# A fused band-attention and feed-forward kernel: softmax sums of the first four tiles from a column of ones in V, a later issue of the range-check reads, and a new set of order tables

## The chip, the cores and the metric

The kernel runs on one core of one Trainium2 chip. The metric is the device time of one execution in microseconds (us), the median of several runs. The engines are named as in the profile: PE (TensorE, matrix products), PEld (its weight loads), DVE (VectorE), ACT (ScalarE), POOL (GpSimd), and SP, whose queue issues nearly all DMAs.

## The reference, cut to what matters

```python
def _attn_ref(q, k, v, n_global, n_local):          # q, k, v: (4, 8, 768, 64) float32
    scores = scale * np.matmul(q, k.transpose(0, 1, 3, 2))
    is_global = pos[None, :] < int(n_global)         # 8
    is_local = (rel >= 0) & (rel < int(n_local))     # 96
    dist = np.where(is_global & ~is_local, float(n_local), np.abs(rel))
    scores = scores - slopes[:, None, None] * dist   # slopes 2 ** -(h + 1)
    scores = np.where(is_global | is_local, scores, -1e9)
    a = np.exp(scores - np.max(scores, axis=-1, keepdims=True))
    a = a / (np.sum(a, axis=-1, keepdims=True) + 1e-09)
    return np.matmul(a, v)

def _moe_ref(x, g_ln, w_ch1, w_ch2):                 # x: (4, 768, 512); 512 -> 2048 -> 512
    xn = (x - mu) / np.sqrt(var + 1e-06) * g_ln
    return x + np.maximum(xn @ w_ch1, 0.0) @ w_ch2   # weights arrive as float64
```

## The kernel before

The 3072 tokens are cut into 24 tiles of 128. Tiles 0 to 3 are the first tile of each batch: they see one block of keys and are computed in float32. Tiles 4 to 23 see two blocks and are computed in float16 pairs (a high and a low part). Two tiles make a chunk c of 256 tokens for the feed-forward part: chunk 0 is tiles 0 and 1, chunk 1 is tiles 2 and 3, and so on. From chunk 3 on (`EVEN`) the second product is computed by seven block products in place of eight.

**Names.** For tile t and group of heads g the tasks are: `S` scores (PE), `R` mask and minimum (DVE), `E` exponentials (ACT), `tp`/`pl` transpose of the weights on PE and its copy to SBUF (tiles 0 to 3), `ph`, `pl`, `pt` split and transposing DMA (other tiles), `P` weights by values (PE), `Z`/`X` divisor and division (ACT, DVE), `B`, `A`, `W`, `C` the statistics and normalisation, `xt`, `xh`, `xl` transpose and the two halves of xT (tiles 0 to 3), `xa` the same by a DMA (other tiles). `F` is the first product of the feed-forward part (in the trace PE writes `f` from `xT` and `w1h`, `w1l`), `G` and `N` the second (`f` from `w2`, and `m`). A weight piece n of 16 passes through `wb` (load), `wr` (ACT, `less`), `ws` and `ww` (DVE, int32), `wu` (`w1h` or `w2h`) and `wl` (DVE, `w1l` or `w2l`). Pieces 0 to 7 are w1, two pieces for every two F of each chunk; pieces 0 to 3 stand in the room of `w2h` and `w2l` until then, so their `wr`, `ws` and `ww` rows read `w2h<-w2h` and `w2l<-w2l`. `gk` copies 16 keys between tiles (DVE, `kT<-kT`).

**What sets the order.** Every engine works strictly in the order in which its instructions were written. That order comes from a planner (class `Plan`): each task has a cost, a rank and the tasks it waits for, and the planner starts, on each engine, the ready task of lowest rank. Ranks come from the step at which a task is due, plus table entries: `FIRST` and `KINDS` by kind, `SHIFT` by task; `GIVEN` fixes the engine of a task that two engines could do. Where the planner sees PE idle before its time `UNTIL`, it writes filler products (`blank`) of 128x512 that nobody reads; they are there to keep PE at work. The PE order of the steps themselves is fixed by code: four F of chunk 0, two of chunk 1, two of chunk 0 and so on (`TURN`). The eleventh F in that order, F0_12, is the first that needs weight pieces 6 and 7.

**The sum before.** For tiles 0 to 3 an exponential row of one head is one ACTIVATE on ACT with `accum_out=sm`, which puts an ACTIVATION_READ_ACCUMULATOR behind it. One division by the eight sums then makes x.

**The range check.** Near the end the float64 weights are read once more (`again`, 64 reads of 256 KB, tasks `V0` to `V63`), each followed by a DVE pass (`J`, tile `seen`). They share 12 buffers. The result decides whether a general path must run instead.

## Time and profile before

| what | value |
|---|---|
| median of 3 runs | 599.83 us (599.55 to 600.0) |
| the profiled execution | 599.55 us |
| its span, first to last instruction | 597.8 us |
| PE busy | 586.9 us (98%) |
| DVE, ACT, POOL busy | 494.0, 429.3, 154.0 us |
| granted TensorE clock | 1.0 throughout, the 2.4 GHz level |

The profiled execution lies 1.75 us above its span (the launch around the instructions) and 0.28 us below the median. The busy shares are means over stages: DVE is full in the first quarter and has room later, PE is filled with filler products in the first 44 us.

### The profile page before, as it was taken

Reading aid. Unit: us, or ns where it says so; the run is one execution under the profiler, and the core shown is the slowest. Engines: PE = TensorE matmul, PEld = TensorE weight load, DVE = VectorE, ACT = ScalarE, POOL = GpSimd, SP = SyncE. Lnnn points to the kernel's source line nnn. Section 1 sums busy time; section 2 is a strip of 40 time slices with the busy share of each in tenths; the row PEclk is TensorE's granted clock in tenths of the full one; section 3 lists DMA queues with packets and bytes.
Section 4 is the critical chain, followed back from the end, with each engine's and each line's share of the span. In section 5 each row is a group of like instructions: output and inputs, shape, how many; then the busy total and the mean of one; then the engine's idle time right before and its main releaser. Section 6 shows DMA issues by size and latency. Waiting matters only on the chain. (4 is left out here: it accounts for less than half of the span.)

```text
span 597.8 us, 15687 instructions
## 1 busy us (share of the span) xinstructions
PE 586.9 (98%) x5982; PEld 494.9 (83%) x5982; DVE 494.0 (83%) x1207; ACT 429.3 (72%) x1092; POOL 154.0 (26%) x133
## 2 busy tenths in 40 slices
PE   8999999999999999999999999999999999999996
PEld 5768895547956899999999999999999999888885
DVE  3899999989898987887887886877976876699994
ACT  5999697767666897797787698899686675623330
POOL 2322032135363253231330130231330420300100
PEclk9999999999999999999999999999999999999999
DMA  8995989999966848797776789759569646999931
GB/s 218 332 311 134 249 202 271 248 173 194 181 135 124 187 89 147 159 166 159 169 115 127 138 154 169 174 121 175 111 140 170 118 91 72 233 280 278 393 107 39
DMA packets 256754, 105.40 MB, mean 176 GB/s; under 512 B 238372, under 2 KB 238628, under 8 KB 256676
## 3 DMA queue, kind: packets, MB, share of 16 engines
q1 hardware_dynamic: 256672, 104.37, 78.1%
q8 instruction: 48, 0.79, 0.5%
q14 instruction: 30, 0.25, 0.1%
q10 hardware_dynamic: 4, 0.00, 0.0%
HBM read 54.53 MB, written 6.29 MB: 102 GB/s over the span
## 5 line engine op out<-in xcount | busy, mean ns | idle before, releaser
L257 PE MATMUL f<-xT,w1h 128*128 128x256 f16 x1536 | 256.3, 273 | 1.6 <-DMA xT<-xn 0.9
L257 PE MATMUL f<-xT,w1l 128*128 128x256 f16 x768 | 209.3, 273 | 0.0
L257 PEld LDWEIGHTS <-w1h 128*128 128x128 f16 x1536 | 147.3, 98 | 18.0 <-DMA xT<-xn 1.1
L257 ACT ACTIVATE uh<-R 128x896 f16<-128x896 f32 x72 | 67.9, 943 | 51.8 <-DVE R L257 50.3
L257 PEld LDWEIGHTS <-uh 128*128 128x128 f16 x1008 | 96.2, 98 | 10.5
L257 DVE SCALAR_TENSOR_TENSOR R<-f,R 128x128 f32<-128x128 f32 (+1 forms) x216 | 72.1, 334 | 20.6 <-ACT R L257 15.6
L257 PEld LDWEIGHTS <-w1l 128*128 128x128 f16 x768 | 75.1, 98 | 9.6 <-issue 0.7
L257 ACT ACTIVATE T<-T,mn 128x256 f32<-128x256 f32 x160 | 80.0, 500 | 4.3 <-ACT mn L257 0.4
L257 DVE TENSOR_TENSOR ul<-R,uh 128x896 f16<-128x896 f32 x60 | 68.1, 1136 | 17.0 <-ACT uh L257 15.9
L257 POOL TENSOR_TENSOR pn<-T,pn 128x512 f16<-128x512 f32 x37 | 49.9, 1349 | 120.2 <-ACT pn L257 82.4
L257 PE MATMUL m<-w2h,uh 128*128 128x256 f16 x288 | 78.5, 273 | 0.0
L257 PE MATMUL m<-w2l,uh 128*128 128x256 f16 x288 | 78.5, 273 | 0.0
L257 PE MATMUL m<-w2h,ul 128*128 128x256 f16 x288 | 78.5, 273 | 0.0
L257 PE MATMUL m<-t,uh 128*128 128x256 f16 x432 | 78.3, 273 | 0.0
L257 DVE CUSTOM_DVE_ANT_0 T<-s,mask 128x256 f32<-128x256 f32 (+1 forms) x192 | 68.1, 395 | 8.6 <-PE s L257 8.6
L257 PE MATMUL f<-w2h,h 128*128 128x512 f16 x192 | 60.1, 379 | 0.0
L257 PE MATMUL m<-t,ul 128*128 128x256 f16 x216 | 58.9, 273 | 0.0
L257 PE MATMUL s<-kT,qT 128*128 128x128 f16 (+1 forms) x704 | 56.9, 225 | 0.7 <-DVE kT L257 0.7
L257 PEld LDWEIGHTS <-ul 128*128 128x128 f16 x504 | 49.3, 98 | 5.7
L257 ACT ACTIVATE mn<-nm 128x2 f32<-128x2 f32 x80 | 15.8, 198 | 53.2 <-DVE nm L257 52.9
L257 POOL TENSOR_TENSOR rs<-rs,half 128x1 f32<-128x1 f32 x24 | 18.2, 760 | 138.1 <-DVE rs L257 138.0
L257 PEld LDWEIGHTS <-h 128*128 128x128 f16 x288 | 27.3, 98 | 29.7
(144 smaller groups left out, 994.6 us busy)
## 6 DMA issues: line engine op xcount, KB each, us to landing
again<-in_moe_w_ch_dram SPq DMA_DIRECT2D x64, 256.0 KB, 5.1
st<-in_moe_w_ch_dram SPq DMA_DIRECT2D x10, 1024.0 KB, 6.0
vf<-in_v_dram SPq DMA_DIRECT2D x28, 256.0 KB, 3.4
kf<-in_k_dram SPq DMA_DIRECT2D x28, 256.0 KB, 4.0
qf<-in_q_dram SPq DMA_DIRECT2D x24, 256.0 KB, 3.7
out_dram<-x SPq DMA_DIRECT2D x23, 256.0 KB, 3.6
qT<-qT SPq DMA_DIRECT2D x40, 128.0 KB, 3.5
w2h<-in_moe_w_ch_dram SPq DMA_DIRECT2D x3, 1024.0 KB, 6.6
```

Source lines behind the costliest of these rows:

```text
L257: ins = getattr(self.engine, name)(*args, **kw)
```

## The change

Four things are changed.

- `HALVES = 1`. For tiles 0 to 3 the V tile is loaded 65 columns wide per head, POOL writes ones into the last column (`one`), and the product with V gives the sum of the weights as its 65th column. The exponentials lose `accum_out`. The product of each half of the heads has a PSUM tile of its own, and so the divisor (`Za`, `Z`) and the division (`Xa`, `X`) are done in two halves.
- The reads `V12` to `V63` of the range check name the task `J` that frees their buffer and get 2.5 us of slack in the planner, so that they are written later in SP's order.
- The tables `FIRST`, `SHIFT`, `MARGIN`, `GIVEN` and `lag` have new values. The constants `EARLY` and `FAVOR` change too, but PE's planned time starts at 1.5 and is never below `EARLY`, so `FAVOR` is not used.
- `GIVEN`, empty before, names an engine for 62 tasks.

```diff
-HALVES = 0
+HALVES = 1
...
 GIVEN = {
-
+    "mask0_4": "DVE", "mask0_1": "DVE", "mask0_5": "DVE", "mask0_7": "DVE", "mask1_3": "ACT", "mask1_5": "ACT", "mask1_6": "ACT", "wu4": "ACT",
...
-    def __init__(self, lag=0.039):
+    def __init__(self, lag=0.038):
...
-        task(f"V{n_}", "SP", 0.6, lambda n_=n_, tag=tag: read_again(n_, tag), [f"S{B * NT - 1}_1"], rank=1e4 + n_, take={tag: [f"J{n_}"]}, dma=0.8)
+        task(f"V{n_}", "SP", 0.6, lambda n_=n_, tag=tag: read_again(n_, tag), [f"S{B * NT - 1}_1"] + ([f"J{n_ - 12}"] if n_ >= 12 else []), rank=1e4 + n_, take={tag: [f"J{n_}"]}, dma=0.8, slack=2.5 * (n_ >= 12))
```

Of the code that `HALVES` switches on, these lines matter:

```python
act.activation(out=T[:, u, :], in_=T[:, u, :], func=AF.Exp, scale=-1.0, bias=mn[:, h:h + 1])
sums[t, g] = (ps_f if g else ps_v).tile([P, gh, D + 1], F32, tag="f2" if g else "pv", name=f"pv{t}_{g}")
pv, r, x_, sum_ = sums.pop((t, g))[:, :, :D], made["r", t][:, g::2], x[:, g::2, :], made["sum", t] if g else 0.0
act.activation(out=made["r", t][:, g::2], in_=sums[t, g][:, :, D], func=AF.Copy, bias=1e-9)
```

Over the whole main path the change in instruction counts is: PE 7 fillers fewer (66 to 59), 56 of the 59 ahead of the first F against 65 before; on ACT 8 small divisors (`r<-pv`) for 4, `w1h` 4 more, masks of 128x256 5 more, masks of 128x128 4 fewer; on POOL masks 7 to 1, `pn` 37 to 43, `kn` 11 to 7; on DVE `pn` 43 to 37, `kn` 13 to 17, 8 half divisions for 4 whole ones.

ACT's order near its start, where the exponentials of tile 0 stand (`T_0` and `T_1` are its two groups). Before:

```order
L257 ACTIVATE kT_0_174<-tk_167 128x512
L257 ACTIVATE mask_87<-d_158 128x128 x8
L257 ACTIVATE T_0_200,sm<-T_0_200,nm 128x128 x4
L257 ACTIVATE T_1_218,sm<-T_1_218,nm 128x128 x4
L257 ACTIVATE pT_0_251<-tp_0_239 128x512
L257 ACTIVATE r<-sm 128x8
```

And of the change:

```order
L265 ACTIVATE kT_0_171<-tk_164 128x512
L265 ACTIVATE mask_87<-d_160 128x128 x4
L265 ACTIVATE mask_88<-d 128x256 x3
L265 ACTIVATE T_0_200<-T_0_200,nm 128x128 x4
L265 ACTIVATE T_1_214<-T_1_214,nm 128x128 x4
L265 ACTIVATE pT_0_243<-tp_0_238 128x512
```

The exponentials no longer write `sm`; half of the small masks went to DVE, and three of the wide masks came from POOL.

DVE's order ahead of the `w1l` of weight pieces 6 and 7, which F0_12 waits for. Before:

```order
L257 SCALAR_TENSOR_TENSOR h_8_929<-f_0_8_867,h_8_929 128x512
L257 SCALAR_TENSOR_TENSOR st_849<-st_849 128x1024 x2
L257 SCALAR_TENSOR_TENSOR h_10_963<-f_0_10_902,h_10_963 128x512
L257 SCALAR_TENSOR_TENSOR w1l<-w2h,gw,w1h 128x512 x2
L257 SCALAR_TENSOR_TENSOR w1l<-st_849,gw,w1h 128x512 x2
L257 SCALAR_TENSOR_TENSOR h_4_998<-f_1_4_936,h_4_998 128x512
```

And of the change:

```order
L265 TENSOR_TENSOR kn_1_908<-kf_1_756,kn_1_908 128x8x64
L265 SCALAR_TENSOR_TENSOR w1l<-w2h,gw,w1h 128x512 x2
L265 SCALAR_TENSOR_TENSOR h_8_939<-f_0_8_876,h_8_939 128x512
L265 SCALAR_TENSOR_TENSOR h_10_975<-f_0_10_913,h_10_975 128x512
L265 SCALAR_TENSOR_TENSOR qn_945<-qf_2_597,qn_945 128x8x64
L265 SCALAR_TENSOR_TENSOR st_830<-st_830 128x1024
L265 SCALAR_TENSOR_TENSOR w2l<-w2l 128x1024
L265 SCALAR_TENSOR_TENSOR h_4_1011<-f_1_4_949,h_4_1011 128x512
L265 SCALAR_TENSOR_TENSOR w1l<-st_830,gw,w1h 128x512 x2
```

The second pair of `w1l` stands behind `h_4` of chunk 1 now, and behind one int32 pass of a later weight piece (`w2l<-w2l`).

SP's order at the range-check reads, with the transposing DMAs of tile 23 (`pT_1`, `pT_2`) between them. The difference:

```order
L257 DMA_TRANSPOSE pT_1_8430<-pn_1_8365 128x8x128
L257 DMA again_8465<-in_moe_w_ch_dram 128x256
L257 DMA again_8470<-in_moe_w_ch_dram 128x256
L257 DMA again_8473<-in_moe_w_ch_dram 128x256
L257 DMA again_8476<-in_moe_w_ch_dram 128x256
L257 DMA_TRANSPOSE pT_2_8489<-pn_2_8467 128x8x128
```

```order
L265 DMA_TRANSPOSE pT_1_8449<-pn_1_8381 128x8x128
L265 DMA again_8481<-in_moe_w_ch_dram 128x256
L265 DMA again_8488<-in_moe_w_ch_dram 128x256
L265 DMA again_8490<-in_moe_w_ch_dram 128x256
L265 DMA_TRANSPOSE pT_2_8502<-pn_2_8484 128x8x128
```

Three reads stand between the two transposes of the change, four stood there before (the first of each pair is the kernel before, the second the changed one).

## Rows read from the trace of the kernel before

**Rows 1.** Busy time by stage: stretch, its length, busy us (count) of each engine, PEclk, DMA, GB/s.
```profile
10.80:44.71 33.91, 32.61 (x231) 24.74 (x231) 29.84 (x100) 33.03 (x106) 11.83 (x12) 1.00 1.01 312
44.71:72.12 27.41, 27.36 (x254) 24.52 (x254) 26.48 (x35) 21.97 (x36) 4.21 (x3) 1.00 0.78 196
72.12:112.12 40.00, 39.30 (x352) 27.36 (x351) 39.78 (x75) 33.09 (x73) 9.66 (x6) 1.00 0.96 232
```

**Rows 2.** Waits of PE: who waited for whom, us in total, times, longest.
```profile
PE pv L257 <- DMA pT<-pn: 1.0, 2, 0.5
PE f L257 <- DMA xT<-xn: 0.9, 1, 0.9
PE s L257 <- DVE kT L257: 0.7, 1, 0.7
```

**Rows 3.** Timeline of PE before the first F: start, us, instruction, count [idle before].
```profile
42.22 1.89 PE L257 MATMUL blank<-ident 128*128 128x512 f16 x8
...
44.76 0.27 PE L257 MATMUL f<-xT,w1h 128*128 128x256 f16 x1 [0.54 <-DVE xT L257]
```

**Rows 4.** Timeline of ACT, 9 to 46 us.
```profile
9.00 1.69 ACT L257 ACTIVATE mask<-d 128x128 bf16<-128x128 f32 x8
10.80 0.40 ACT L257 ACTIVATE T<-T,nm 128x128 f32<-128x128 f32 x1
11.11 0.19 ACT L257 ACTIVATION_READ_ACCUMULATOR T<-T,nm 128x1 f32 x1
11.21 0.39 ACT L257 ACTIVATE T<-T,nm 128x128 f32<-128x128 f32 x1
...
37.96 1.21 ACT L257 ACTIVATE w2l<-w2l,less 128x1024 int32<-128x1024 uint32 x1
39.06 0.57 ACT L257 ACTIVATE pT<-tp 128x512 f32<-128x512 f32 x1
...
39.86 0.81 ACT L257 ACTIVATE xs<-x,off,rs 128x512 f32<-128x512 f32 x1
...
42.22 0.57 ACT L257 ACTIVATE xT<-tx 128x512 f16<-128x512 f32 x1
...
45.09 1.40 ACT L257 ACTIVATE w1h<-w2l,gw 128x512 f16<-128x512 f32 x2
```

**Rows 5.** Timeline of DVE, 29 to 45 us.
```profile
29.54 1.85 DVE L257 TENSOR_SCALAR w1h<-w2h,gw 128x512 f16<-128x512 f32 x2
...
39.20 3.94 DVE L257 SCALAR_TENSOR_TENSOR w2l<-w2l 128x1024 int32<-128x1024 int32 x2 [0.36 <-ACT w2l L257]
43.06 0.20 DVE L257 RECIPROCAL r<-r 128x8 f32<-128x8 f32 x1
43.41 0.69 DVE L257 CUSTOM_DVE_ANT_1 x<-pv,r 128x512 f32<-128x512 f32 x1
...
44.02 0.69 DVE L257 TENSOR_TENSOR xT<-tx,xT 128x512 f16<-128x512 f32 x1
```

**Rows 6.** Timeline of POOL at the same place.
```profile
38.91 1.90 POOL L257 TENSOR_TENSOR w1h<-w2l,gw 128x1024 f16<-128x1024 f32 x1
```

**Rows 7.** Timeline of DVE, 59 to 73 us.
```profile
59.72 2.32 DVE L257 SCALAR_TENSOR_TENSOR w1l<-st,gw,w1h 128x512 f16<-128x512 f32 x2
...
63.76 2.47 DVE L257 SCALAR_TENSOR_TENSOR w2h<-w2h 128x1024 int32<-128x1024 int32 x2
...
71.07 1.41 DVE L257 SCALAR_TENSOR_TENSOR w1l<-st,gw,w1h 128x512 f16<-128x512 f32 x2
```

**Rows 8.** Timeline of DVE, then of SP's queue, ahead of the wait at 139.6 us.
```profile
135.08 0.68 DVE L257 TENSOR_TENSOR xn<-xs,xn 128x512 f16<-128x512 f32 x1
...
135.79 1.23 SPq L257 DMA_TRANSPOSE xT<-xn  x1
```

**Rows 9.** Timeline of SP's queue, 518 to 523 us.
```profile
518.76 2.75 SPq L257 DMA_DIRECT2D again<-in_moe_w_ch_dram  x4
521.61 1.30 SPq L257 DMA_TRANSPOSE pT<-pn  x1
```

More of the change, by code (lines that the diff above doesn't have):

```diff
@@ L81 @@
 EVEN = 3
-EARLY = -18.5
+EARLY = -20
 LEAD = 4
@@ L90 @@
 VLATE = 0.0
-FAVOR = {"ACT": 36.8, "POOL": -10.6}
+FAVOR = {"ACT": 60.9, "POOL": -11.1}
 LATER = {"ACT": -1.68, "POOL": -0.05}
@@ L95 @@
 TAIL = {"PE": 0.16, "ACT": 0.1, "DVE": 0.09, "POOL": 0.06}
-MARGIN = {"ACT": 0.0126, "DVE": 0.0032, "POOL": 0.091}
+MARGIN = {"ACT": 0.0316, "DVE": 0.0, "POOL": 0.075}
 SPLIT = 190.0
 FIRST = {
[4 rows of a table removed]
[4 rows of a table added]
 }
```

40 rows, old and new, of tables (FIRST, GIVEN, SHIFT) are left out of this document.

## The prediction

> **What bounds the kernel now.** I read the busy time by stage first, then PE's waits, and then the timelines at the places where PE waits. From 44.76 us on PE works on products that count, and it is all but full: after that moment its waits are 0.7 us for a copy of keys, 0.9 us for an xT that a DMA brings, and twice about 0.5 us for a pT, 2.6 us together [rows 2]. So the kernel has two parts. What comes after 44.76 us can shrink by 2.6 us at most, since no product is taken away. What comes before, 44.76 us, ends when DVE has written the second half of xT for tile 1: PE's first F waits for it [rows 3]. In that stretch PE is busy only because fillers stand there; ACT works 33.03 of 33.91 us and DVE 29.84 [rows 1]. The stage behind it matters too: from 44.71 to 112.12 us DVE works 66.26 of 67.41 us [rows 1], and it is DVE that PE then waits for.
>
> **The change up to the first F.** The path is shared by ACT and DVE, so I add up both queues, each from the first exponential or mask to the xT of tile 1. An ACTIVATE's price is the distance to the next start, its length less 0.09 us (10.80 + 0.40 against 11.11); the accumulator read behind it adds 0.10 (11.11 to 11.21) [rows 4].
>
> ACT needs 31.4 us from 10.80 to 42.22 [rows 4]. Gone are 32 accumulator reads. Their price has a lower bound of 0.10 each, 3.2 us, if the exponential keeps its length; the upper bound is the distance of the small masks, 0.20 each (1.69 us for 8), against 0.39 for an exponential with its read, 6.1 us. I take 3.2, since the exponential's own row is the nearest. By the order of ACT's instructions these change as well ahead of the xT of tile 1: two copies of 0.48 fewer (a pT is one), -1.0; three small `r` of 0.1 more, +0.3; one `less` pass more, +1.1; four `w1h` halves more, +2.6; one normalisation `xs` with its offset fewer, -1.0; two wide masks of an estimated 0.3 more, +0.6 [rows 4]. Sum: -0.6 us; with the upper bound -3.5. ACT's half of the xT ended at 42.79 and would end at 42.2, 1.8 us before DVE began its own half at 44.02 [rows 4, 5].
>
> DVE needs 33.55 us from its first mask to 44.02. More: a copy of 0.6, a wide mask of about 0.3, one int32 pass of 1.2, and seven half divisions in place of four whole ones. A whole one costs 0.96 (43.06 to 44.02), of which 0.35 is the reciprocal and its wait; a half I put at 0.35 + 0.31, an estimate with half of the elements, so 4.6 against 3.8, +0.8. Less: the two `w1h` of 1.85, which ACT takes [rows 5]. Sum: +1.05. Then there is POOL. The two int32 passes at 39.20 took 3.94 us, and at 63.76 two of the same shape took 2.47 [rows 5, 7]; beside the slow ones POOL ran `w1h<-w2l` for 1.90 us from 38.91 [rows 6]. That POOL instruction is gone, and six of seven masks on POOL with it: -1.5. DVE's own work is then 0.4 us shorter. It also idles about 4 us in this stretch (29.84 of 33.91, [rows 1]), one of them just ahead of the slow passes and waiting for ACT [rows 5], and of these waits an ACT that is earlier gives some back.
>
> So ACT allows 1.8 us, and DVE allows 0.4 plus what it idles less: DVE sets it. I take 1.3 us for the start of the first F (0.9 of the 4 us of idle time go), with bounds of 0.3 (no wait goes) and 2.5 (ACT far ahead by the upper bound, half of the idle time gone). The order gives one more number to hold against it: 9 fillers fewer stand ahead of the first F, at 0.22 us each (42.22 to 43.95 for 8), so PE may come 1.9 us earlier and no more unless they were hiding waits [rows 3]. The memsets of ones on POOL have no price: four of them, in an engine that works 11.83 of 33.91 us [rows 1].
>
> **The change after the first F.** Three places follow in time.
>
> *F0_12, now at about 72 us.* Its second `w1l` pair ended at 72.48 [rows 7], that is 28.4 us after DVE began the xT of tile 1, and PE came just then. Counted out with 0.60 for a pass of 512 columns, 1.33 for a pair of `w1l` and 1.13 for an int32 pass, DVE's rows between these two points came to 26.6 us before and come to 28.0 now: the half division of tile 3, an int32 pass of another piece and `h_4` of chunk 1 stand in between. The 1.8 us that the trace shows above 26.6 are waits and a POOL pass beside DVE (2.32 us for a pair of `w1l` at 59.72 against 1.41 at 71.07) [rows 7]. With the same 1.8 PE gets there 1.4 us late; with none of them DVE is in time, and PE loses the net two fillers that stand there now, 0.4 us. I take 1.0.
>
> *The key copy at 111.6 us.* DVE's work ahead of it is 2.0 us less than before by the same count (66.3 us from the xT of tile 1, before 68.3). PE comes 1.0 us later. The wait of 0.7 goes [rows 2].
>
> *The xT of chunk 2 at 139.6 us.* `xn` of tile 5 ended at 135.76, its DMA was issued at 135.79 and PE began at 140.50 [rows 8, 2]. What is late next shows here: DVE has 1.2 us more ahead of this `xn` than before, its waits in the same chain (behind two key and value passes) are about 1 us shorter, and PE comes 0.3 us later on balance (1.0 - 0.7). Bounds: the wait stays as it is less 0.3, or grows by 0.9. I take +0.2.
>
> *The end.* PE's second wait of 0.5 us for a pT comes behind four range-check reads, which SP issued in 2.75 us [rows 9]. One of the four is moved behind the pT: 0.7 us sooner, and the wait of 0.5 goes. The first wait stays, since the eight reads ahead of it stay. The later reads move by 2.5 us at most, and nothing but the verdict waits for them. I take -0.5, with bounds of 0 and -1.0.
>
> In between, from 140.5 to 522 us, PE waits for nothing in the trace; DVE gets 3 to 4 us more work there and ACT 8 us less. I take 0, and up to 1.0 lost.
>
> **Sum.** -1.3 + 1.0 - 0.7 + 0.2 - 0.5 = -1.3 us, on the profiled execution of 599.55: 598.25, so 598.2. The median of the runs shown is 0.28 above that execution. A change of under 0.2%, 1.2 us, counts as no change here.
>
> **The Trainium skill on a price.** The Trainium skill, "SBUF — State Buffer", section "Who interferes with whom", says that a DVE instruction with two SBUF inputs and a GpSimd instruction that reads SBUF exclude each other for a whole instruction. The 3.94 us beside 1.90 agree with it. By that rule the six `pn` that go from DVE to POOL relieve DVE of nothing, since POOL's pass holds it up for longer than its own would last; this is rival B below.
>
> **Rivals.**
>
> *A. No change.* The longer chain of the sums (product, divisor, two divisions in place of one) keeps DVE waiting for all its 4 us, F starts 0.3 us earlier, F0_12 costs 1.0, the key copy and the pT give 1.2 back. 599.55 - 0.3 + 1.0 + 0.2 - 1.2 = 599.3. For it: DVE's work does not shrink. Against it: ACT, the fuller of the two [rows 1], gets room.
>
> *B. Slower: DVE falls behind.* From 44.71 to 112.12 us DVE has 1.15 us of room [rows 1], and the change gives it no less work in all. If POOL's added passes hold DVE up, as the pair at 59.72 shows with 0.9 us each, it loses the 1.8 us at F0_12 and as much again ahead of the xT of chunk 2. It decides from the point where DVE loses 1.5 us more than before between the first F and 140 us. Price: -0.3 (first F) + 1.4 + 1.8 - 0.5 = +2.4, 601.9 at the worst and 600.9 with half of the second loss.
>
> *C. Much faster.* The exponentials cost 0.20, the first F starts 2.5 us earlier, F0_12 loses only its fillers, 0.4, and all four waits go, 2.6 less a remainder of 0.6: 599.55 - 2.5 + 0.4 - 2.0 = 595.45.
>
> **Chances and range.** The forecast 0.45, A 0.18, B 0.20, C 0.17. A quarter of the forecast's share lies above 598.35, within 0.2% of the time before. So faster by over 0.2%: 0.33 + 0.17 = 0.50; within: 0.12 + 0.18 = 0.30; slower: 0.20. The range takes in C but for its end and B up to half of its second loss: 595.5 to 600.9. The forecast's own range is 597.2 to 599.0.
>
> **What would show it.** The exponentials of tiles 0 to 3 should follow each other at 0.30 us, or at 0.20 if the upper bound holds. The first F should wait for DVE's xT still, with its dense start near 43.4 us. PE's waits should name `w1l` near 71 us, no `kT`, one xT by DMA of about a microsecond and one pT. The prediction is wrong if the first F starts after 44.4 or before 42.2, or if PE's waits after it are above 3.5 us.

## The result, and the profile after

| | median | ratio to the kernel before, 95% interval |
|---|---|---|
| kernel before, beside it | 600.0 us (599.55 to 601.37, 5 runs) | |
| changed kernel | 605.85 us (604.05 to 607.11, 5 runs) | 1.0093 [1.0077, 1.0109] |

The change makes the kernel slower by 0.9%, 5.6 us, where 1.3 us faster was forecast. Later runs were made on several chips, on which the median of the kernel before lay between 599.7 and 601.4 us; they are compared by their ratio to it.

The profiled execution of the changed kernel took 605.07 us (span 603.3). Its busy time by stage, in the windows of [rows 1], and PE's clock in 2 us windows where it fell:

```profile
10.80:44.71 33.91, 30.48 (x222) 23.12 (x221) 29.84 (x102) 32.13 (x78) 7.64 (x7) 1.00 1.06 314
44.71:72.12 27.41, 26.66 (x247) 23.79 (x245) 23.27 (x35) 20.93 (x36) 3.31 (x3) 1.00 0.76 183
72.12:112.12 40.00, 38.61 (x334) 26.60 (x333) 38.39 (x68) 28.60 (x66) 11.47 (x9) 0.96 0.92 221
...
74.00:76.00 2.00, 1.05 (x5) 0.53 (x6) 2.00 (x4) 0.45 (x1) 0.00 (x0) 0.77 0.76 172
76.00:78.00 2.00, 2.00 (x12) 1.43 (x10) 2.00 (x7) 1.10 (x4) 0.00 (x0) 0.50 1.18 254
78.00:80.00 2.00, 2.00 (x22) 1.75 (x21) 1.39 (x2) 1.55 (x5) 1.06 (x1) 0.88 0.96 335
```

DVE is no longer full behind the first F (23.27 of 27.41 us, 26.48 before), and between 72 and 112 us the clock is no longer 1.00. In 76:78 PE is busy all the time and gets through 12 instructions at the lower level (0.50, 1.2 GHz) where 78:80 shows 22 at 0.88.

PE's waits, as in [rows 2]:

```profile
PE pv L265 <- DVE mv L265: 2.9, 1, 2.9
PE tx L265 <- DVE r L265: 2.6, 1, 2.6
PE f L265 <- DMA xT<-xn: 2.0, 3, 1.0
...
PE f L265 <- DVE w1l L265: 1.2, 1, 1.2
PE s L265 <- DMA qT<-qT: 0.7, 1, 0.7
...
PE f L265 <- ACT w1h L265: 0.2, 1, 0.2
```

The kT wait and both pT waits of [rows 2] are gone. What is new is 2.9 us for `mv`, 2.6 for `r` (it stands before the first F), 2.1 in three waits near 72 us, and two further waits for an xT, 1.0 together, the longer of them far behind the rest:

```profile
234.80 0.39 PE L265 MATMUL f<-xT,w1h 128*128 128x256 f16 x2 [0.75 <-DMA xT<-xn]
```

**Where the time went.** Executions differ by up to 2.2 us in when their first exponential starts, also with the same instructions ahead of it on ACT (9.42 to 11.59 us in the changed kernel and the runs below that keep its order there). So I count from that start, between moments that every trace shows: first F (its first product with `w1l`), first G (first product with `w2`), first F of chunk 2, first product into `m`, start of the last product.

| us | to first F | to first G | to F2_0 | to first m | to the end | sum |
|---|---|---|---|---|---|---|
| before | 34.07 | 45.33 | 50.30 | 64.71 | 387.18 | 581.59 |
| after | 34.74 | 50.07 | 49.42 | 66.95 | 387.14 | 588.32 |
| difference | +0.67 | +4.74 | -0.88 | +2.24 | -0.04 | +6.73 |

Three places lose: a little before the first F, most between first F and first G, the rest between F2_0 and the first m. One gains, 0.88 between first G and F2_0, of which 0.70 is the kT wait that is gone. Each loss has its rows.

*23 to 28 us.* DVE's pair of int32 passes, POOL's pass beside it, and PE:

```profile
23.08 4.07 DVE L265 SCALAR_TENSOR_TENSOR w2h<-w2h 128x1024 int32<-128x1024 int32 x2
23.25 2.81 POOL L265 TENSOR_TENSOR w1h<-w2h,gw 128x1024 f16<-128x1024 f32 x1 [1.79 <-DVE gw L265]
27.90 0.63 PE L265 MATMUL tx<-ident,xs 128*128 128x128 f32 x4 [2.57 <-DVE r L265]
```

This answers to [rows 5, 6]: the pair took 3.94 there beside 1.90 of POOL. The same meeting has only moved, from a place where PE had fillers to one where it waits. The exponentials themselves follow each other at 0.30, as forecast from [rows 4]:

```profile
9.85 2.45 ACT L265 ACTIVATE T<-T,nm 128x128 f32<-128x128 f32 x8
```

*55 to 75 us.* SP's queue, then ACT, DVE and PE:

```profile
55.82 2.26 SPq L265 DMA_DIRECT2D st<-in_moe_w_ch_dram  x2
58.72 1.44 SPq L265 DMA_TRANSPOSE kT<-kn  x1
61.19 4.17 SPq L265 DMA_TRANSPOSE qT<-qn  x1
65.45 1.26 SPq L265 DMA_TRANSPOSE kT<-kn  x1
...
68.91 1.20 SPq L265 DMA_DIRECT2D qT<-qT  x2
...
66.55 0.63 ACT L265 ACTIVATE qn<-qf 128x512 f16<-128x512 f32 x1 [1.73 <-DMA kT<-kn]
68.92 0.63 ACT L265 ACTIVATE kn<-kf 128x512 f16<-128x512 f32 x1 [1.74 <-DMA qT<-qn]
...
70.07 0.69 DVE L265 SCALAR_TENSOR_TENSOR h<-f,h 128x512 f16<-128x512 f32 x1 [3.51 <-ACT h L265]
74.15 1.41 DVE L265 SCALAR_TENSOR_TENSOR w1l<-st,gw,w1h 128x512 f16<-128x512 f32 x2
...
71.97 0.55 PE L265 MATMUL s<-kT,qT 128*128 128x128 f16 x7 [0.75 <-DMA qT<-qT]
73.37 0.39 PE L265 MATMUL f<-xT,w1h 128*128 128x256 f16 x2 [0.20 <-ACT w1h L265]
74.95 0.32 PE L265 MATMUL f<-xT,w1l 128*128 128x256 f16 x1 [1.18 <-DVE w1l L265]
```

The rows read as a chain. Two 1 MB reads (pieces 6 and 13) are issued 1.9 us apart. Behind them stand the transposing DMAs of tile 4: that of its first keys (58.72) lands 7.7 us after its issue, that of its queries takes 4.17 us to issue, and that of its other keys starts only at 65.45. ACT waits twice for the buffers which the first two of these DMAs read; `h` behind it is late; DVE waits 3.51 us for that `h`; so the second `w1l` pair, at 71.07 in [rows 7], begins at 74.15. PE waits for the copies of `qT`, for `w1h` and for `w1l`. In the kernel before the read of piece 13 was issued at 95.12. The link between the read and the slow issue is the firmest part of this chain: in the six traces in which the read stands there (the changed kernel, fillers, POOL to DVE, casts to ACT, gw later, reads back) the queries' transposing DMA takes 3.37 to 4.50 us to issue, and in the nine of the runs below that move the read it takes 1.23 in each.

*184 to 199 us.* DVE, POOL and PE:

```profile
184.27 1.53 DVE L265 TENSOR_TENSOR pn<-T,pn 128x512 f16<-128x512 f32 x1
185.72 1.37 DVE L265 CAST t<-va 128x512 f16<-128x512 f32 x1
187.13 1.53 DVE L265 TENSOR_TENSOR t<-va,t 128x512 f16<-128x512 f32 x1
...
191.05 1.31 DVE L265 CAST kn<-kf 128x512 f16<-128x512 f32 x1
192.39 1.53 DVE L265 TENSOR_TENSOR kn<-kf,kn 128x512 f16<-128x512 f32 x1
193.84 1.64 DVE L265 SCALAR_TENSOR_TENSOR qn<-qf,qn 128x512 f16<-128x512 f32 x1
...
185.21 1.60 POOL L265 TENSOR_TENSOR va<-va,w2h 128x512 f32<-128x512 f32 x1
186.78 1.33 POOL L265 TENSOR_TENSOR va<-va,w2l 128x512 f32<-128x512 f32 x1
...
198.96 0.51 PE L265 MATMUL pv<-vn,pT 128*128 128x64 f16 x12 [2.89 <-DVE mv L265]
```

Six DVE passes of 0.42 to 0.68 us take 1.31 to 1.64 while POOL works on `va`; above the short lengths that is 5.35 us, ahead of the division that releases `pv`.

### The profile page after: what moved, and what is told of

It reads as the page before. It is cut to its first block, busy times and chain, and to the rows that moved or that the text cites. A ratio compares the mean times of both kernels' runs of the same rounds, so it can differ in the third digit from the quotient of the medians.

```text
span 603.3 us, 15657 instructions
## 1 busy us (share of the span) xinstructions
PE 586.4 (97%) x5975; PEld 494.8 (82%) x5975; DVE 507.4 (84%) x1237; ACT 420.4 (70%) x1048; POOL 158.3 (26%) x135
## 5 line engine op out<-in xcount | busy, mean ns | idle before, releaser
L265 POOL TENSOR_TENSOR pn<-T,pn 128x512 f16<-128x512 f32 x43 | 59.5, 1385 | 155.5 <-ACT pn L265 131.2
L265 ACT ACTIVATE uh<-R 128x896 f16<-128x896 f32 x70 | 65.9, 941 | 34.8 <-DVE R L265 34.7
L265 DVE TENSOR_TENSOR ul<-R,uh 128x896 f16<-128x896 f32 x59 | 65.9, 1116 | 15.0 <-ACT uh L265 14.3
L265 ACT ACTIVATE R<-f 128x512 f32<-128x512 f32 x70 | 40.9, 585 | 31.3 <-PE f L265 26.4
L265 POOL TENSOR_TENSOR rs<-rs,half 128x1 f32<-128x1 f32 x24 | 19.8, 824 | 117.9 <-DVE rs L265 105.9
```

The costliest lines, as they stand in the source:

```text
L265: ins = getattr(self.engine, name)(*args, **kw)
```

## The experiments

Most edits change only the place of a task in the finished order (`MOVED`: a task, and the task that it is put behind), or its engine (`ON`), by lists that are applied behind the planner; nothing else moves:

```diff
+        for key, behind in MOVED:
+            row = order.pop([k for _, k, _ in order].index(key))
+            order.insert([k for _, k, _ in order].index(behind) + 1, row)
...
-(lambda fn=fn, engine=engine: fn(engine))
+(lambda fn=fn, engine=ON.get(key, engine): fn(engine))
```

The stages of all runs, counted as above:

| run | ratio [interval] | to first F | to first G | to F2_0 | to first m |
|---|---|---|---|---|---|
| later load | 1.0106 [1.0084, 1.0128] | 35.62 | 47.67 | 50.35 | 68.63 |
| fillers | 1.0134 [1.0111, 1.0157] | 35.61 | 48.15 | 49.99 | 69.83 |
| POOL to DVE | 1.0057 [1.0043, 1.0072] | 37.26 | 48.19 | 49.70 | 65.83 |
| casts to ACT | 1.0080 [1.0061, 1.0099] | 35.62 | 49.19 | 49.72 | 67.97 |
| spread load | 1.0155 [1.0121, 1.0188] | 35.61 | 45.90 | 57.77 | 66.94 |
| gw later | 1.0059 [1.0036, 1.0081] | 33.62 | 48.50 | 49.70 | 68.28 |
| three edits | 1.0074 [1.0049, 1.0099] | 33.46 | 45.72 | 56.77 | 65.76 |
| sums only | 1.0242 [1.0209, 1.0275] | 35.77 | 45.19 | 59.04 | 67.45 |
| three moves | 1.0029 [1.0009, 1.0050] | 33.48 | 47.17 | 49.41 | 69.15 |
| reads only | 0.9999 [0.9979, 1.0019] | 34.47 | 45.29 | 49.79 | 65.18 |
| reads back | 1.0127 [1.0083, 1.0171] | 38.20 | 48.32 | 49.78 | 68.42 |
| all places | 1.0001 [0.9988, 1.0013] | 33.49 | 46.86 | 50.79 | 65.13 |
| all places, reads back | 1.0057 [1.0039, 1.0074] | 41.23 | 46.50 | 50.26 | 65.10 |
| no sums | 1.0401 [1.0378, 1.0424] | 43.86 | 50.56 | 60.51 | 64.81 |
| all places 2 | 1.0003 [0.9982, 1.0023] | 33.45 | 45.23 | 53.62 | 64.98 |
| load after pT | 1.0103 [1.0080, 1.0127] | 36.39 | 45.91 | 50.78 | 66.95 |
| spaced | 1.0059 [1.0036, 1.0081] | 33.47 | 45.22 | 54.67 | 67.44 |

### The early read

```diff
+MOVED = [("wb13", "kt5_2"), ("wr13", "hh0_14")]
```

> Changed kernel, with one 1 MB weight read moved back on SP's queue: the read of piece 13 goes from its place ahead of tile 4's transposing DMAs (second st read at 55.82 us) to behind those of tile 5, and its ACT pass goes back behind h_14 of chunk 0. Nothing else moves. Theory (a full DMA queue): the transposing DMA of tile 4's queries, 4.17 us of issue at 61.19, falls to about 1.3; ACT's two waits of 1.73 and 1.74 for buffers of transposing DMAs shrink to under 1 us together; PE's waits at 72 to 75 us (0.75, 0.20, 1.18) go, and with them the fall of the granted clock to 0.50 in 76:78, worth 1.6 us. Gain 2.1 + 1.6 = 3.7: 602.1 against 605.85. Rival 1 (the prediction's own term: DVE has too much work ahead of w1l of piece 6): the wait for w1l stays near 1 us, the clock still falls, gain about 1: 604.9. Rival 2 (something behind takes the gain, since DVE is nearly full up to 199 us): the waits at 72 go, but the wait of 2.89 at 196 grows by as much: 605.5 or so.

Half right. SP's and PE's rows of this run:

```profile
63.84 1.23 SPq L276 DMA_TRANSPOSE qT<-qn  x1
...
73.63 0.58 SPq L276 DMA_DIRECT2D st<-in_moe_w_ch_dram  x1
...
76.22 0.53 SPq L276 DMA_DIRECT2D st<-in_moe_w_ch_dram  x1
...
79.33 6.01 SPq L276 DMA_TRANSPOSE pT<-pn  x1
...
88.31 0.52 PE L276 MATMUL pv<-vn,pT 128*128 128x64 f16 x12 [1.58 <-DMA pT<-pn]
```

The queries' transposing DMA takes 1.23 us to issue, PE has no wait between 60 and 80 us, and the clock stays at 1.00 there. But the read now stands 2.6 us ahead of that of piece 10, and the next transposing DMA, a pT, takes 6.01 us to issue. PE waits for it at 88 us. From the first F to the first G this trace is 2.4 us shorter than the changed kernel's. But the clock fell in 28:36, behind PE's wait for `r`, and again behind the wait for `mv` (0.65 in 200:204), neither of which this edit touches: 0.9 us more to the first F, 1.7 more from F2_0 to the first m. No gain in the time, neither by 3.7 as the theory had it nor by 1.

The whole chain of piece 13 moved back as far as in the kernel before:

```diff
+MOVED = [(a + "13", a + "12") for a in ("wb", "wr", "ws", "ww", "wu", "wl")]
```

> Changed kernel with the whole chain of weight piece 13 (its 1 MB read, its pass on ACT, three passes on DVE, one more on ACT) moved back from its early place to directly behind the same step of piece 12, some 40 us later, where the kernel before has it too. Theory (1 MB reads that stand 2 to 3 us apart fill the DMA queue, and the transposing DMA behind them pays): with one early read less, no transposing DMA between 55 and 100 us takes over 3 us to issue; the gap at 72 to 75 us goes as it did in the run with the later read (PE's waits there 0, clock 1.00 in 70:80), and the new gap that stood at 88 us there (1.58 for a pT, 2.71 of DVE for h) does not come. First G about 3.7 us earlier against the first F than in the changed kernel. If all of it reaches the end: ratio to the kernel before 1.003. Rival (DVE sets the pace up to 199 us and takes the gain back at the division of tile 8): gaps gone as above, wait at 196 us 4 us or more, ratio 1.007 to 1.010.

To the first G the theory holds (45.90). Behind it neither theory does: with the passes of piece 13 late, its buffer is free late, the read of piece 15 waits for it at the head of SP's queue (11.5 us, until it is issued at 116.16), and the pT behind that read costs PE 4.46 us at 122 us. The next two runs put the read where the most time is to spare:

```diff
+MOVED = [("wb13", "pt4_2"), ("wr13", "wr11"), ("ws13", "ws11")]
```

> The changed kernel with that one move alone (read of piece 13 behind the third pT of tile 4, with its two passes). It measures what the early read costs in the changed kernel when no other transposing DMA pays for it. Theory (the read makes the gap at 72 to 75 us): PE's waits between 60 and 80 us gone, clock 1.00 there, first F to first G 45.7 us against 50.1 (46 to 48 in runs with the gap but without a fall of the clock: 48.2 to 49.2). If the gain lasts: 2.5 to 4 us, ratio to the kernel before 1.003 to 1.005. Rival (taken back where DVE is the bound): the wait at 196 us 4 us or more, ratio 1.008 or above.

From the first F to the first G it is 45.91 us, against 48.2 to 50.1 in the runs with the gap. Yet the ratio is no better. The trace is that of its fastest execution (602.6; the other five took 605.6 to 608.1), in which PE still waits 2.91 at 28 us, 1.28 for a small copy into `vn` at 108 and 2.88 near 197. What the slower executions lost isn't shown by a trace; their mean granted clock was 0.990 to 0.993, against 0.996 in this one, which over 600 us is 1.8 to 3.6 us of clock (an estimate), beside the 3.0 to 5.5 us by which they were slower.

### The clock

```diff
+EXTRA = {"hh1_6": 0, "wl6": 3, "S4_0": 6}
```

> Changed kernel with nine more filler products on PE where it waits at 71 to 75 us: three ahead of the first scores of tile 4, six ahead of F0_12. No data arrives earlier. Theory (the clock falls because PE stood idle 2.1 us of 4): PE works through the gap, the granted clock stays 1.00 in 70:80, F0_12 still ends its wait at about 74.95, and the 1.6 us lost to the lower level come back: 604.2 against 605.85. Rival 1 (the level falls for another reason): 76:78 still shows about 0.5, time 605.85 to 606.4, since the fillers can only delay. Rival 2: the clock holds but the wait of 2.89 us at 196 grows by the same 1.6, since DVE sets X of tile 8: 605.9.

`EXTRA` gives the number of fillers that PE gets behind a task. The clock is 1.00 in 70:80 with PE busy 9.88 us of the 10 (7.87 at 0.83 in the changed kernel). But the four other traces with the gap unmended (POOL to DVE, casts to ACT, gw later, reads back) show 1.00 there as well; in the first two PE is busy only 0.62 and 0.69 us of 76:78. So a gap doesn't always bring the clock down, and this run can't prove that the fillers kept it up. The 1.6 us weren't gained: the wait for `mv` is 4.4 us (2.9 before the edit), as the second rival had it. In the time the run is worse than that rival: 1.0134, an interval above that of the changed kernel. Its trace has a fall of the clock behind that wait (0.62 in 200:204) and 1.99 us of waiting for an xT at 240 us.

### POOL beside DVE

```diff
+ON = {"yl1_1": "DVE", "ya20_3": "DVE", "ya12_0": "DVE", "yl4_2": "DVE"}
```

> Changed kernel with four passes of the w2 combinations (POOL at 184.09, 185.21, 186.78, 190.91 us) done by DVE at the same place of the order. DVE gets 4 x 0.61 = 2.4 us more work ahead of the division of tile 8, for which PE waits 2.89 us at 196. Theory (POOL and DVE keep each other out): the six DVE passes that took 1.31 to 1.64 in place of 0.42 to 0.68 between 184 and 196, 5.35 us too long together, fall back to their short length; DVE reaches the division 2.9 us earlier, the wait goes to about 0: 603.0 against 605.85; with the two POOL passes that stay still in the way of two DVE passes, 604.2. Rival (POOL's help is help, and the long passes have another cause): DVE is 2.4 us later and the wait is 5.3: 608.3.

The sharpest test: DVE gets more work and is done sooner. Five of DVE's six passes from the rows at 184 to 199 us above:

```profile
188.57 0.42 DVE L276 CAST t<-va 128x512 f16<-128x512 f32 x1
189.03 0.69 DVE L276 TENSOR_TENSOR t<-va,t 128x512 f16<-128x512 f32 x1
...
192.71 0.42 DVE L276 CAST kn<-kf 128x512 f16<-128x512 f32 x1
193.16 0.69 DVE L276 TENSOR_TENSOR kn<-kf,kn 128x512 f16<-128x512 f32 x1
193.78 0.69 DVE L276 SCALAR_TENSOR_TENSOR qn<-qf,qn 128x512 f16<-128x512 f32 x1
```

These and the sixth (0.69 at 187.96) are back at 0.42 and 0.69. The wait for `mv` is 1.77, the stage to the first m 65.83 (66.95 in the changed kernel), and the ratio lies below that of the changed kernel with no overlap. The Trainium skill, "SBUF — State Buffer", section "Who interferes with whom", says that casts too can take the port pair that DVE shares with GpSimd, and that whoever comes second waits for the other's whole instruction. The casts at 1.31 and 1.37 in place of 0.42, and the recovery here, agree.

```diff
+ON = {"ph9_0": "ACT", "yh2_2": "ACT", "qh11": "ACT", "kh11_3": "ACT"}
```

> Changed kernel with four casts that the new table gives to DVE (pn of tile 9, t of block row 2, qn and kn of tile 11; DVE at 183.82, 185.72, 190.03, 191.05) done by ACT, which stands idle 5.79 us at 184.4 to 190.2. Theory (DVE is the bound from 145 to 199 us and was given too much): DVE loses 1.4 us of work if the long passes only move to the next instruction, 3.3 if the long casts go whole: wait at 196 between 0 and 1.5, time 603.0 to 604.4 against 605.85. Rival (ACT's casts come late because they stand behind casts that wait for DVE): DVE waits for ACT in their place, time 605.3 to 606.5.

The wait for `mv` falls to 2.24, by 0.65 and not by 1.4 or more, and two waits for a pT, 1.0 together, come in. The ratio can't be told from that of the changed kernel. By the wait (2.24 against 1.77), taking work from DVE helped less than taking POOL out of its way; the intervals of the two ratios overlap.

```diff
+MOVED = [("gw", "ww1")]
```

> Changed kernel with one 0.17 us instruction of DVE moved: gw, for which POOL's w1h pass waits, goes behind the pair of int32 passes of piece 1 instead of ahead of it. So POOL's pass (2.81 us at 23.25) can no longer run beside that pair (4.07 us at 23.08 in place of 2.36). Theory (the two keep each other out, and PE's wait of 2.57 us for r at 25.3 comes from it): the pair takes 2.4 us, PE's wait for r falls to about 0.9, the granted clock stays at 1.00 in 20:44, and the first F starts 1.5 us or more earlier than in runs with that wait (44.4 without and 46.8 to 47.9 with a fall of the clock). Ratio to the kernel before 1.0065, or 1.004 where the clock had fallen. Rival 1 (POOL's pass meets the next DVE instructions instead, and wl0 waits for it): first F as before, 1.009. Rival 2 (the gap at 72 us takes it back): first F earlier, ratio 1.009.

```profile
22.18 2.48 DVE L276 SCALAR_TENSOR_TENSOR w2h<-w2h 128x1024 int32<-128x1024 int32 x2
24.82 1.90 POOL L276 TENSOR_TENSOR w1h<-w2h,gw 128x1024 f16<-128x1024 f32 x1 [3.75 <-DMA vf<-in_v_dram]
25.57 0.66 PE L276 MATMUL tx<-ident,xs 128*128 128x128 f32 x4 [0.64 <-ACT xs L276]
```

The pair takes 2.48 us, POOL's pass 1.90, and PE's wait for `r` is gone (0.64 for ACT stays). The first F comes 33.62 us behind the first exponential, 1.1 earlier than in the changed kernel. Ratio 1.0059: the theory holds, though the interval touches that of the changed kernel.

### The sums and the reads by themselves

```diff
-HALVES = 0
+HALVES = 1
...
-            task(f"Z{t}", "ACT", 0.1, lambda: divisor(1), [last], rank=rank - 4)
+            task(f"Z{t}", "ACT", 0.1, lambda: divisor(1), [last, f"Za{t}"], rank=rank - 4)
```

> The kernel before with its own tables and its own range-check reads, and only the new sums switched on (HALVES = 1, with one dependency that keeps the two divisors of a tile in order). The planner writes a new order from the old tables. By the prediction's own steps: exponentials at 0.30 us each, first F 1.3 us earlier, the divisions in halves cost DVE 0.8: ratio 0.998. Rival 1 (the tables, not the sums, made the loss): ratio 0.996 to 1.003, no gap at 72 to 75 us. Rival 2 (the sums made the loss, since DVE's longer chain is late whatever the order): waits of PE before and at 70 us as in the changed kernel, ratio 1.007 or more.

None of the three: the ratio, 1.0242, is above the 1.007 of rival 2, but not through the waits that it names. The first G is on time (45.19), but the order that the planner makes of the old tables lets PE wait 3.05 and 4.60 us for two pT at 144 to 149 us, and the clock is at 0.50 in 148:152. The other half, the new tables without the sums:

```diff
-HALVES = 1
+HALVES = 0
```

> The changed kernel's tables, engine table and range-check reads, with the new sums switched off (HALVES = 0, as in the kernel before). The planner writes a new order; the 1 MB read of piece 13 still stands directly behind that of piece 6 and ahead of tile 4's transposing DMAs. Theory (the tables put the reads side by side, and that fills the queue whatever the sums do): a transposing DMA of 4 us or more of issue between 55 and 65 us, a gap of PE between 65 and 80 us, ratio to the kernel before 1.008 or more. Rival 1 (the gap needs the sums' later DVE): no wait of PE of over 1 us between 60 and 80 us, ratio 1.002 to 1.006. Rival 2 (the loss came with the sums): ratio 1.002 or less.

```profile
56.29 1.66 SPq L265 DMA_DIRECT2D st<-in_moe_w_ch_dram  x2
62.51 4.28 SPq L265 DMA_TRANSPOSE kT<-kn  x1
...
162.72 0.80 PE L265 MATMUL pv<-vn,pT 128*128 128x64 f16 x12 [8.37 <-DVE pn L265]
```

A transposing DMA of 4.28 us behind two reads, as the theory had it, but PE's gap at 69.91 us, 1.07, is for the xT of the next chunk and not for tile 4, and most is lost at 163 us, 8.37 for a pn of DVE. The tables belong to the code that they were made for; neither run measures the sums or the tables.

```diff
-[f"S{B * NT - 1}_1"], rank=1e4 + n_, take={tag: [f"J{n_}"]}, dma=0.8)
+[f"S{B * NT - 1}_1"] + ([f"J{n_ - 12}"] if n_ >= 12 else []), rank=1e4 + n_, take={tag: [f"J{n_}"]}, dma=0.8, slack=2.5 * (n_ >= 12))
```

> The kernel before with its own sums and tables and only the changed line of the range-check reads. SP's order changes in two places (two reads go behind the transposing DMA of tile 23 and further), DVE's passes over them follow. Prediction's step: PE's second wait for a pT (0.49 at 525 us) goes, the first (0.46) stays: 0.5 us, ratio 0.999, not to be told from no change by the times but by PE's waits. Rival 1: both waits stay, since transposing DMAs are as late whatever stands between: 1.000. Rival 2: the later reads end behind the last product, and the verdict makes the end later: 1.001 or more.

0.9999. Both waits of 522 and 525 us are gone, and one of 0.50 for a pT stands at 534 us: 0.45 less, the forecast size, though not in the way forecast (the first wait was to stay). It isn't to be seen in the times, as expected, nor in the stage from the first m to the end, 387.45 us against 387.18.

The accumulator reads put back, in the order of the run with gw later:

```diff
-act.activation(out=T[:, u, :], in_=T[:, u, :], func=AF.Exp, scale=-1.0, bias=mn[:, h:h + 1])
+act.activation(out=T[:, u, :], in_=T[:, u, :], func=AF.Exp, scale=-1.0, bias=mn[:, h:h + 1], accum_out=sm[:, h:h + 1])
```

> The changed kernel with gw later, in the same order, but with the accumulator reads of the 32 exponentials of tiles 0 to 3 put back (the sums that they write are not used). So ACT gets 32 x 0.10 = 3.2 us more between 10 and 40 us and nothing else differs. It measures what the sums out of V save on the path to the first F, whose start is at 42.9 us in the run with gw later. Prediction's step (ACT and DVE share the path, the reads are worth 1.3 us of the 3.2): first F at 44.0 to 44.5. Rival 1 (ACT is the path all the way): 3.2 later, 46.1. Rival 2 (DVE is the path): under 0.4 later, 43.3 at most. Times follow the first F, if the gaps behind it don't move with it: ratio 1.008, 1.011 or 1.006.

The ratio is 0.0068 higher, 4.1 us, and the first F 4.6 us later, more than any of the three; the clock had fallen at 16:24 us. So the same was tried on a better base (below).

### All places together

```diff
+MOVED = [("wb13", "wb12"), ("wr13", "wr12"), ("ws13", "ws12"), ("ww13", "ww12"), ("wu13", "wu12"), ("wl13", "wl12"), ("gw", "ww1")]
+ON = {"yl1_1": "DVE", "ya20_3": "DVE", "ya12_0": "DVE", "yl4_2": "DVE"}
```

> Changed kernel with three of the edits at once: the chain of piece 13 behind that of piece 12, gw behind the int32 pair, and four POOL passes of 184 to 191 us done by DVE. Theory (three separate places, each a gap of PE): gains add up, 3.7 + 1.5 + 1.5 of the 605.85: 599.2, ratio 0.999, PE's waits after the first F under 3 us and the clock at 1.00 up to 590 us. Rival (DVE is the bound from 45 to 199 us and the gains are given back at its last long stage): first F and first G early, but the wait near 196 us at 4 us or more, ratio 1.004 or above.

Up to the first G this is ahead of the kernel before (33.46 + 45.72 = 79.2 us, 79.4 before), and then the read of piece 15 blocks SP as above: 4.54 us for a pT at 118, clock at 0.53 in 120:124. The wait for `mv` is 1.71, so it isn't the rival's either.

```diff
+MOVED = [("gw", "ww1"), ("wb13", "qt4"), ("wr13", "hh1_6"), ("P8_3", "G4_14"), ("X8", "ql11")]
```

> Changed kernel with three instructions or groups moved and nothing else: gw behind the int32 pair of piece 1 (as in the run with gw later, ratio 1.006); the early 1 MB read of piece 13 behind the transposing DMA of tile 4's queries instead of ahead of it and of the keys' one (its pass on ACT behind h_6 of chunk 1); and the division of tile 8 on DVE ahead of pn of tile 9, two sums into x and the next minimum, 2.6 us earlier in DVE's order. Theory (each gap of PE is one instruction that stands behind others in a queue): the wait for qT and w1l at 70 to 75 us goes, 2.1 us; the wait for mv near 196 us falls from 2.9 to about 0.3; no fall of the clock at either place (up to 1.5 us); first F at 43 us as with gw later. Against the 603.6 of that run: 603.6 - 2.1 - 2.6 - 1.0 = 597.9, ratio to the kernel before 0.997. Rival 1 (the 1 MB read holds up another transposing DMA instead, as it did at 79 and at 112 us when it was moved further): a new wait for pT of 1.5 us or more, ratio 1.003 or above. Rival 2 (DVE is the bound): the gap at 72 goes, but the wait near 196 stays above 2, ratio 1.004.

1.0029. The wait for `w1l` is gone, that for the copies of `qT` is 1.30, since the read now stands ahead of them. At 194 us the wait for `mv` falls to 0.79, but 0.93 for a pT and 1.35 for what the division had overtaken follow, and the clock falls to 0.60 in 200:204. By its letter rival 2 (a wait above 2) isn't met; in sum it is, 3.07 us in the three. Moving one division in DVE's order moved the wait to what it overtook.

```diff
+MOVED = [("gw", "ww1"), ("wb13", "qa4"), ("wr13", "hh0_14")]
+ON = {"yl1_1": "DVE", "ya20_3": "DVE", "ya12_0": "DVE", "yl4_2": "DVE", "yh2_2": "ACT", "qh11": "ACT"}
...
+        i = [k for _, k, _ in order].index("S4_0") + 1
+        order = order[:i] + [row for row in order[i:] if row[1] != "blank"]
```

> Changed kernel with the three lossy places mended at once, each in the way that has worked alone: gw behind the int32 pair; the early 1 MB read of piece 13 behind the copies of tile 4's queries (its pass on ACT behind h_14 of chunk 0), and the three fillers ahead of F0_12 left out; four POOL passes of the w2 combinations on DVE, and two of DVE's casts ahead of them (t of block row 2, qn of tile 11) on ACT. By stages, from the first exponential: to the first F 33.5 us, from there to the first G 45.4, to F2_0 49.6, to the first m 65.3, to the last product 386.8, together 580.6 against 581.6 in the trace of the kernel before and 588.4 in that of the changed kernel. Theory (these places are the loss): ratio to the kernel before 0.998. Rival 1 (the read fills the queue for the transposing DMAs of tile 5 or the pT at 79 us): first F to first G 47 us or more, ratio 1.001 or above. Rival 2 (DVE sets the stage from F2_0 to the first m whatever is moved): that stage 67 us or more, ratio 1.001 to 1.003.

Ratio 1.0001: the 5.6 us are gone, though the theory's 0.998 lies outside the interval. Sum of the stages 582.6; PE's longest waits that remain:

```profile
83.49 0.52 PE L274 MATMUL pv<-vn,pT 128*128 128x64 f16 x12 [1.47 <-DMA pT<-pn]
92.55 0.38 PE L274 MATMUL f<-w2h,h 128*128 128x512 f16 x1 [1.20 <-DVE h L274]
140.67 0.39 PE L274 MATMUL f<-xT,w1h 128*128 128x256 f16 x2 [1.00 <-DMA xT<-xn]
193.73 0.51 PE L274 MATMUL pv<-vn,pT 128*128 128x64 f16 x12 [1.07 <-DVE mv L274]
```

Rival 1 is there in part: 46.86 us to the first G, with a pT that takes 5.07 us to issue behind reads at 66.9 and 75.1.

> The kernel of the run with all three places mended, with the 32 accumulator reads put back on ACT (the sums that they write are not used): 3.2 us more on ACT between the first exponential and the first F, nothing else changed. The first run of this kind had a fall of the clock at 16 to 24 us in its trace, so that its 4.6 us could not be read. Prediction's step (1.3 of the 3.2 us are on the path): first exponential to first F 34.8 us against 33.5, ratio 0.002 above the run without. Rival 1 (ACT is the path): 36.7 us, ratio 0.005 above. Rival 2 (DVE is the path): under 33.9, no difference in the ratio.

(The same edit as in the run with the reads back.) The ratio is 0.0056 higher, 3.4 us. Part of it is the clock: the trace fell in an execution of 607.7 us whose clock was at the lower level from 16 to 32 us, behind 0.45 us of idle PE in 12:16, so its stage to the first F can't be read. But two of the six executions had a mean granted clock of 0.999 and 1.000, as the kernel without the reads has. They took 603.07 and 601.85 us, 3.2 and 1.9 above the median of that kernel. So most of ACT's 3.2 us seems to be on the path, more than the 1.3 of the prediction; two executions are few, and whether it is on the path in full, as the first rival had it, isn't settled.

```profile
12.00:16.00 4.00, 3.55 (x24) 2.49 (x22) 1.97 (x9) 4.00 (x16) 0.00 (x0) 1.00 1.20 305
16.00:20.00 4.00, 4.00 (x20) 3.63 (x20) 1.65 (x13) 2.09 (x8) 0.00 (x0) 0.55 1.27 264
```

```diff
-MOVED = [("gw", "ww1"), ("wb13", "qa4"), ("wr13", "hh0_14")]
+MOVED = [("gw", "ww1"), ("wb13", "pt4_2"), ("wr13", "wr11"), ("ws13", "ws11")]
```

> As the run with all three places mended, but the early 1 MB read of piece 13 stands behind the third pT of tile 4, some 20 us later on SP, where nothing but loads and transposing DMAs with time to spare follow within 6 us; its pass on ACT stands behind that of piece 11 and its first int32 pass on DVE behind that of piece 11. Theory (the wait of 1.47 for a pT at 83 us and of 1.20 for h at 92 us there came from three 1 MB reads within 21 us): no transposing DMA between 55 and 86 us above 3 us of issue, both waits gone; from the first F to the first G 45.0 us (46.9 there), from there to F2_0 49.5, the other stages as there; sum 579.5, ratio to the kernel before 0.9965. Rival (DVE sets that stretch): both waits gone, but F2_0 waits longer, sum 581.5 or more, ratio 0.999 to 1.001.

The rival's numbers (583.7, 1.0003), but not its reason. To the first G 45.23, both waits gone, but PE then waits 3.51 us at 108 for the small copy into `vn`, which SP issues behind the read at 97.47; that is a DMA and not DVE. Two more reads were moved out of the way:

```diff
-MOVED = [("gw", "ww1"), ("wb13", "pt4_2"), ("wr13", "wr11"), ("ws13", "ws11")]
+MOVED = [("gw", "ww1"), ("wb13", "pt4_2"), ("wr13", "wr11"), ("ws13", "ws11"), ("wb12", "gv0_2"), ("wb15", "pt5_2")]
```

> As the second run with all three places mended, with two more 1 MB reads moved on SP: that of piece 12 behind the small copy into vn of tile 6, and that of piece 15 behind the second pT of tile 5, so that these three DMAs stand ahead of a read and not behind one. Theory (what PE waited for at 104 to 108 us there, 3.51 for vn with a fall of the clock behind it, is the queue filled by the reads at 85.6 and 97.5): the wait goes, F2_0 comes 50 us after the first G (53.6 there), sum of the stages 580.0 against 581.6 before, ratio to the kernel before 0.997. Rival (seven 1 MB reads and the attention's transposing DMAs between 72 and 120 us fill the queue in any order): a wait of 1.5 us or more at another place in that stretch, for a pT or through ACT's pass over piece 12, ratio 0.999 or above.

The rival holds (1.0059). The wait for `vn` is gone; ACT waits 3.80 us for the data of piece 15, DVE 3.84 behind it, and PE 3.85 for xT at 144 us. No version tried beats the kernel before.

## Why the prediction was wrong

By its own sign (PE's waits behind the first F above 3.5 us) the prediction is wrong: they come to 7.0.

**The first F, -1.3: wrong by 2.0.** It came 0.67 us later behind the first exponential; in the trace it starts 0.28 earlier only because the first exponential does by 0.95, which differs from execution to execution. The step that failed reads "That POOL instruction is gone, and six of seven masks on POOL with it: -1.5". Another `w1h` pass of POOL was left, and it met another int32 pair, whose price I had in [rows 5, 6] and didn't look for again. Without the meeting the stage is 33.5 to 33.6 us (six traces), 0.5 better than before and still short of the 1.3. The reads themselves were sized rightly, 0.10 each, and the trace shows the 0.30. A second step failed with the first, "DVE sets it": in the run with all places the reads, put back on ACT, cost 1.9 and 3.2 us in the two executions with a steady clock. Then ACT's other changes ahead of the first F cost more than I took; where the missing 0.8 went isn't shown.

**F0_12, +1.0 (0.4 to 1.4): the largest error.** The stage lost 4.74: 2.13 in three waits, 0.44 in two fillers more, and 2.2 in the same 450 products, most of it behind the fall of the clock; six triplets of F0_12, from 75.06 to 78.75, took 3.69 us where six take 1.97 at the full clock. The place was right, `w1l` near 71 us (it is 74.15), and the count of DVE's rows too: DVE had time for 3.5 us of waiting. What failed was to count DVE alone. The table moved a 1 MB read 37 us ahead on SP, past the transposing DMAs of tile 4, and I priced no DMA of the moved steps. That the read makes the gap is shown by the traces in which it is moved: the queries' transposing DMA takes 1.23 us in all nine, and the wait for that `w1l` is gone in all nine. What that gap is worth in the time isn't: alone, moving the read gave nothing that could be measured (1.0106 and 1.0103 against 1.0093), and the fall of the clock, up to 2.2 us of the stage, came in the changed kernel's trace and in none of the four others with the gap and without the fillers.

**The key copy, -0.7: right.** The wait is gone, though PE came later by more than the forecast had it, so that the sum behind it isn't tested.

**The xT of chunk 2, +0.2:** the wait is 0.99, it was 0.93.

**140.5 to 522 us, 0 (up to 1.0 lost): wrong.** To the first m it lost 2.24, at PE's one wait of 2.89. I had counted DVE's work there (3 to 4 us more) and not whom its passes would meet. This is the mechanism of rival B at a place that B didn't name; its 600.9 to 601.9 (the lower price, with half of the second loss, adds up to 601.05) were too low: two other losses came with it. From the first m to the end the sum hardly changed, -0.04, by luck: a wait of 0.75 for an xT at 235 us, which the forecast didn't have, stands against what was gained at the end.

**The end, -0.5:** both waits of pT are gone in the changed kernel, 0.95; the reads alone gave 0.45.

**What adds up.** The run with all places shows that these places are the loss. If the parts add, then by ratio gw later gave back 0.0034, POOL to DVE 0.0036, and the run with all places 0.0092, the whole loss. The remaining 0.0022, 1.3 us, belong to the read, the fillers and two casts together; the intervals don't divide it further.

## What to carry to other kernels

Where a table moves a load, follow the queue that issues it: list the DMAs that now stand behind it and the engine that waits for their buffers, and price those, not only the bytes. Where passes of two engines stretch each other, as POOL's and DVE's do here, go through the new order pair by pair; a meeting that is removed at one place can turn up at another, and giving work from POOL to a full DVE can make DVE faster. Mending one wait shows what would have been late next: here the read, moved five times, let another DMA pay each time.

## What the runs showed of the hardware

The granted clock falls behind waits of PE, but not behind every one. PE's wait for `mv` near 197 us, 2.2 to 2.9 us long, was followed by a fall (0.57 to 0.69 over 4 us) in the traces of later load, casts to ACT, gw later and reads back, and by none in those of the changed kernel, spread load and load after pT (2.88 to 2.89 us each); the stage to the first m took 68.0 to 68.6 us with the fall and 66.94 to 66.95 without. So one trace of such a kernel can show a loss of over 1 us that the next doesn't have. The same holds for the wait for `r` near 28 us: no fall behind 2.57 us in the changed kernel, falls to 0.50 to 0.93 in 2 us windows behind 2.1 to 2.9 in the six runs in which it stood.
